# Token chunks of 512 instead of 470 in an FFT filter followed by a cosine-gated MLP (one core)

## The chip, the cores and the metric

The kernel runs on one core of one Trainium2 chip. The metric is the device time of one execution in microseconds (us); a smaller number is better. The engines of the core are called PE (TensorE matmul; PEld is its weight load), DVE (VectorE), ACT (ScalarE), POOL (GpSimd) and SP (SyncE, which issues most of the DMAs here).

## The reference

```python
# x: (8, 3008, 256); filt_r, filt_i: (1505, 256); w_in: (256, 2048); w_out: (2048, 256)
X = np.fft.rfft(x, axis=1)
Y = X * (filt_r + 1j * filt_i)[None, :, :]
y = np.fft.irfft(Y, n=3008, axis=1)          # circular filter along the sequence
t = y.reshape(8 * 3008, 256)                 # 24064 tokens
h = t @ w_in
out = (h * np.cos(h)) @ w_out                # (24064, 256), float32
```

## The kernel before

The work has two parts that are interleaved on all engines.

**The filter.** A sequence of 3008 = 47 * 64 positions is transformed by a prime-factor FFT in four stages. Stage 1 (`stage1`, L255) makes the transforms of length 47 and writes them to DRAM as `z1`. Stages 2 and 3 (`stage23`, L286) make the transforms of length 64 forward, multiply by the filter, and go back, to `z2` in DRAM. Stage 4 (`stage4`, L403) loads from `z2` the rows of some of the 64 values n2, multiplies them by a small matrix (L420) and combines even and odd parts (L427 to L429), which gives 47 tokens for each n2. The first sequence (batch 0) goes through faster code of its own (`first1`, `first23`), since nothing else can run before it; the other seven are spread under the second part.

**The MLP.** A chunk of tokens, held as two tiles `y` (a high part `yh`, L432, and the low rest `yl`, L435), goes through eight steps s. In a step, `hidden` (L441) makes 12 matmuls into the PSUM tile `hp`: 256 of the 2048 hidden values for all tokens of the chunk, with three products for each pair of tiles so that the precision is kept. `gate` (L457) then computes h * cos(h): L459 and L460 on DVE (a range reduction), L461 on ACT (a sine), L462 on DVE (the product, which is the last to read `hp`), L465 on ACT (the high part `gh`), L466 on POOL (the low part `gl`). `project` (L469) makes 12 matmuls of `gh` and `gl` into the two PSUM tiles `acc`, two steps after the `hidden` of the same step (`LAG`). After the eighth step L488 and L489 write the result out. A chunk has 470 tokens (five pairs of n2), the last two chunks 282 each: 52 chunks, 416 steps.

PSUM has two `hp` tiles, so the `hidden` of step k + 2 can't start before L462 of step k. The pool `moe` holds three buffers each of `g`, `gh` and `gl`; the pool `ypool` holds the tokens of two chunks.

**Order.** `run_due` hands out parts of the filter between the matmuls of the MLP by a table of due times, counted in slots (eight to a step, `SLOTS`). `LENGTH` slots are used for a sequence, which ends `BEFORE` slots ahead of its first chunk (`LATER` slots less for sequence 1, which can't begin before slot `FIRST`); `BEFORE4` says how far ahead of its use a part of stage 4 runs. A list scheduler of the framework then sets the order of each engine's instructions, and each engine works through its own in that order. The weights are converted on the way (`prep_w`, L199: an ACT instruction L216 after the load, a DVE instruction L219, POOL instructions L220 and L224); their loads stand in SP's queue among the others. Chunk 0 is reached by two parts of stage 4 that run before any MLP step.

Of the kernel before, what the change touches and what calls it, by code (L numbers as in the profile page):

```python
# [10 lines left out]
F32 = mybir.dt.float32  # L11
# [19 lines left out]
SLOTS = 8  # L31
LAG = 2
APART = 3
FIRST, LENGTH, BEFORE = 64, 410, 140
LATER = 28
GAP12, GAP23 = 20, 24
AHEAD1, AHEAD2, AHEAD4 = 28, 28, 24
BEFORE4 = 68
EARLY_W, JUST_W = 9, 5


# [104 lines left out]
def fft_filter_then_cos_glu(ctx: ExitStack, tc: tile.TileContext, ins, outT):
# [41 lines left out]
    chunks = _chunks()  # L188

    @contextmanager  # L190
    def behind():
# [52 lines left out]
    spare = []  # L244

    def psum_f(b):
        if b == 0 and len(done) < 2:
# [120 lines left out]
    def first23(i, fas, fbs):  # L368
        cols = slice(512 * i, 512 * i + 512)
        zf = fft.tile([P, 512], F32, name="zf", tag="ld", bufs=5)  # L370
        nc.sync.dma_start(zf, z1s[0].rearrange("j (h c k) d -> (j h c) (k d)", h=2, c=2)[:, cols])
        yield
        ps = psum_f(0)
        nc.tensor.matmul(ps, mats["f2"], zf, start=True, stop=True)
        half = slice(2 * (i % 2), 2 * (i % 2) + 2)
        ya = fft.tile([P, 512], F32, name="ya", bufs=2)
        yb = fft.tile([P, 512], F32, name="yb", tag="sw", bufs=2)
        for y, f in ((ya, fas), (yb, fbs)):
            nc.vector.tensor_tensor(y, ps, f[i // 2][:, half].rearrange("p k d -> p (k d)"), ALU.mult)
# [12 lines left out]
        to = z2[:NJ].rearrange("j (h c k) d -> (j h c) (k d)", h=2, c=2)[:, cols]  # L392
        n0 = 4 * chunks[0][1]
# [6 lines left out]
    ys = {}  # L400
    done = set()

    def stage4(c, half):  # L403


        j0, n = chunks[c]
        r, w = n * NK, n * Q
        rows = z2.rearrange("j q d -> (j q) d")[j0 * 2 * Q + half * w :][:w]
        zf = fft.tile([P, 2, D], F32, name="z4", tag="ld", bufs=5)[:r]
        load = nc.sync.dma_start(zf, rows.rearrange("(a p) d -> p a d", a=2))  # L410
        if c == 0:
            hold[:] = [load.ins]
        yield
        ps = psum_f(0 if c == 0 else 1)
# [7 lines left out]
        if c not in ys:  # L422
            ys[c] = [ypool.tile([P, NDT, 5 * TJ], F32R, name=f"y{i}") for i in range(2)]
        y = fft.tile([P, NDT, 5, NA], F32, name="y4", bufs=1)[:, :, :n]
        e = v.rearrange("p t (i g n) -> p t i g n", g=2, n=NK)
        odd = fft.tile([P, NDT, 5, NK], F32, name="odd", bufs=1)[:, :, :n]
        nc.scalar.copy(odd, e[:, :, :, 1])  # L427
        nc.vector.tensor_tensor(y[:, :, :, :NK], e[:, :, :, 0], odd, ALU.add)
        nc.vector.tensor_tensor(y[:, :, :, NK:], e[:, :, :, 0, 1:], odd[:, :, :, 1:], ALU.subtract)  # L429
        toks = slice(half * n * NA, (half + 1) * n * NA)  # L430
        yh, yl = (v[:, :, toks].rearrange("p t (i n) -> p t i n", n=NA) for v in ys[c])
        cast = nc.scalar.copy(yh, y)  # L432
        if (c, half) == (0, 1):
            hold.append(cast.ins)
        (nc.vector if c < 2 else nc.gpsimd).tensor_tensor(yl, y, yh.bitcast(F32), ALU.subtract)  # L435
        done.add((c, half))


    gs, accs = {}, {}

    def hidden(c, s):  # L441
        nt = chunks[c][1] * TJ
        yh, yl = ys[c]
        assert {(c, 0), (c, 1)} <= done
        hp = ps_h.tile([P, 2, 512], F32, name="hp")
        for u in range(2):
            fs = slice(u * P, (u + 1) * P)
            for t in range(NDT):
                for n, (w, y) in enumerate(((0, yh), (0, yl), (1, yh))):
                    nc.tensor.matmul(hp[:, u, :nt], w_in[s][w][:, t, fs], y[:, t, :nt],  # L450
                                     start=(t == 0 and n == 0), stop=(t == NDT - 1 and n == 2))
                if u == 0 or t == 0:
                    yield
        with tc.high_priority() if c == 0 else nullcontext():
            gs[c, s] = gate(hp[:, :, :nt], nt)

    def gate(h, nt):  # L457
        g = moe.tile([P, 2, 5 * TJ], F32, name="g")[:, :, :nt]
        nc.vector.tensor_scalar(g, h, 0.25, MAGIC, ALU.add, ALU.add)  # L459
        nc.vector.scalar_tensor_tensor(g, g, MAGIC, h, ALU.subtract, ALU.subtract)  # L460
        nc.scalar.activation(g, g, AF.Sin, bias=half_pi, scale=-TWO_PI)  # L461
        nc.vector.tensor_tensor(g, g, h, ALU.mult)  # L462
        gh = moe.tile([P, 2, 5 * TJ], F32R, name="gh")[:, :, :nt]
        gl = moe.tile([P, 2, 5 * TJ], F32R, name="gl")[:, :, :nt]
        nc.scalar.copy(gh, g)  # L465
        nc.gpsimd.tensor_tensor(gl, g, gh.bitcast(F32), ALU.subtract)  # L466
        return gh, gl

    def project(c, s):  # L469
        nt = chunks[c][1] * TJ  # L470
        if s == 0:
            accs[c] = [ps_o.tile([P, 512], F32, name=f"acc{e}") for e in range(2)]
        gh, gl = gs.pop((c, s))
        for e in range(2):
            acc = accs[c][e][:, :nt]
            es = slice(e * P, (e + 1) * P)
            for u in range(2):
                for n, (w, g) in enumerate(((0, gh), (1, gh), (0, gl))):
# [31 lines left out]
    with tc.tile_pool(name="first", bufs=12) as first, tc.manual_schedule(engines={mybir.EngineType.SP}):  # L510
# [47 lines left out]
    with tc.issue_after(hold[0]):  # L558
        for g in twos:
            next(g, None)  # L560
    steps = [(c, s) for c in range(len(chunks)) for s in range(NS)]

    due = []

# [18 lines left out]
            if pe:  # L583
                last[0] = now

    def slot(j):
        c = max(c for c in range(len(chunks)) if chunks[c][0] <= j)
        return SLOTS * NS * (c + (j - chunks[c][0]) / chunks[c][1])

    for b in range(1, B):  # L590
        end = slot(b * NJ) - BEFORE
        if b == 1:
            end += LATER
        start = max(end - LENGTH, FIRST)
# [7 lines left out]
    for c in range(1, len(chunks)):  # L602
        j0, n = chunks[c]
        for half in range(2):
            at = [SLOTS * NS * (c + (2 * half + t) / 4) - BEFORE4 for t in range(NDT)]
            b = (2 * j0 + (half + 1) * n - 1) // NB
            plan(stage4(c, half), at[0] - AHEAD4, at, lambda b=b: len(wrote2.get(b, ())) == n23)
    due.sort(key=lambda d: d[0])
    for k in range(len(steps) + LAG):
        parts = []  # L610
# [66 lines left out]
```

## Time and profile before

| | |
|---|---|
| median of 3 runs | 2503.86 us (2502.52 to 2504.66) |
| the profiled execution, its own time | 2502.54 us |
| its span, first to last instruction | 2500.4 us |
| mean granted TensorE clock | 0.992 |
| busy: PE, PEld, DVE, ACT, POOL | 2446.8, 2121.9, 1883.6, 1297.5, 1430.7 us |
| MLP matmuls | 9600 of 470 columns, 384 of 282 columns |
| gates | 400 of 128 x 940, 16 of 128 x 564 |

A line of the timeline shows a start time, the time taken, the engine, the source line and operation, output<-inputs by the program's names, shapes, how many were merged, and in brackets the idle time of the engine ahead of it with what ended it. Matmuls overlap, so what a matmul costs is read from the distance of starts and not from its own length.

### The profile page before, as it was taken

The numbers are of one execution on the slowest core, as the hardware profiler recorded it, in microseconds if no ns is written. First come the engines' busy times: TensorE is split into PE (matmuls) and PEld (weight loads), VectorE is DVE, ScalarE is ACT, GpSimd is POOL, SyncE is SP. The second block draws the span as 40 slices with busy tenths as digits, with TensorE's granted clock in tenths as the row PEclk, the third lists the DMA queues.
The fourth block names the chain that finished last, engine by engine and source line by source line (L and its number), as shares of the span: only waits on it lengthen the run. The fifth ranks groups of instructions, "written<-read, shape, count | busy, mean of one in ns | idle before, by whom it ended". The sixth has DMA issues, their size and how long they took to land.

```text
span 2500.4 us, 31920 instructions
## 1 busy us (share of the span) xinstructions
PE 2446.8 (98%) x11743; PEld 2121.9 (85%) x11743; DVE 1883.6 (75%) x2027; ACT 1297.5 (52%) x1751; POOL 1430.7 (57%) x824
## 2 busy tenths in 40 slices
PE   7799999999999999999999999999999999999999
PEld 2578888888888888888888888888888888888888
DVE  2688977887678866888678876788867886666665
ACT  1655554555555554555545564455554554444444
POOL 1776665665566555665556665556555654444444
PEclk8899999999999999999999999999999999999999
DMA  9633343323232132222322223222312221000000
GB/s 319 210 108 122 99 120 88 104 91 92 61 109 90 64 99 80 88 91 75 80 84 95 79 84 92 69 88 79 100 57 80 85 66 49 24 25 14 16 9 18
DMA packets 136301, 212.40 MB, mean 85 GB/s; under 512 B 12786, under 2 KB 77858, under 8 KB 136146
## 3 DMA queue, kind: packets, MB, share of 16 engines
q1 hardware_dynamic: 82526, 138.02, 18.2%
q10 hardware_dynamic: 53620, 72.34, 9.0%
q8 instruction: 94, 1.54, 0.3%
q14 instruction: 61, 0.50, 0.1%
HBM read 135.33 MB, written 74.97 MB: 84 GB/s over the span
## 4 chain that ended last, share of the span: by engine, by line
PE 87%; DVE 6%; DMA 3%; issue 2%; ACT 1%; POOL 1%; SPq 0%; ACTq 0%; POOLq 0%; DVEq 0%
PE hp L450 38%; PE acc L479 38%; PE ps L420 3%; PE ps L236 2%; PE ps L238 2%; PE ps L237 2%; DVE sw L310 1%; DVE g L460 1%; DVE g L459 1%; DVE g L462 1%; DMA zf<-z 1%; ACT g L461 1%; DVE zh L298 0%; DMA xf<-in_x 0%; PE hp L363 0%
## 5 line engine op out<-in xcount | busy, mean ns | idle before, releaser
L466 POOL TENSOR_TENSOR gl<-g,gh 128x940 fp32r<-128x940 f32 (+1 forms) x416 | 918.2, 2207 | 837.0 <-ACT gh L465 583.2
L450 PE MATMUL hp<-y,w_in 128*128 128x470 f32 (+1 forms) x4992 | 1135.1, 375 | 17.3 <-DVE g L462 14.5
L450 PEld LDWEIGHTS hp<-y,w_in 128*128 128x128 f32 x4992 | 925.0, 189 | 147.2 <-issue 9.9
L479 PE MATMUL acc<-gh,w_out 128*128 128x470 f32 (+1 forms) x3328 | 914.3, 373 | 0.3 <-ACT gh L465 0.3
L462 DVE TENSOR_TENSOR g<-g,hp 128x940 f32<-128x940 f32 (+1 forms) x416 | 463.9, 1115 | 335.0 <-ACT g L461 334.4
L479 PEld LDWEIGHTS acc<-gh,w_out 128*128 128x128 f32 x3328 | 619.5, 188 | 82.8 <-ACT gh L465 0.5
L461 ACT ACTIVATE g<-g,half_pi 128x940 f32<-128x940 f32 (+1 forms) x416 | 445.1, 1070 | 462.9 <-DVE g L460 427.6
L465 ACT CAST gh<-g 128x940 fp32r<-128x940 f32 (+1 forms) x416 | 402.1, 967 | 457.7 <-DVE g L462 445.3
L479 PE MATMUL acc<-gl,w_out 128*128 128x470 f32 (+1 forms) x1664 | 569.2, 377 | 4.2 <-POOL gl L466 4.2
L459 DVE TENSOR_SCALAR g<-hp 128x940 f32<-128x940 f32 (+1 forms) x416 | 464.2, 1116 | 112.1 <-PE hp L450 110.4
L460 DVE SCALAR_TENSOR_TENSOR g<-g,hp 128x940 f32<-128x940 f32 (+1 forms) x416 | 463.8, 1115 | 10.7
L479 PEld LDWEIGHTS acc<-gl,w_out 128*128 128x128 f32 x1664 | 311.9, 188 | 46.2 <-POOL gl L466 5.3
L316 POOL TENSOR_TENSOR yl<-ya,yh 128x512 fp32r<-128x512 f32 x84 | 113.5, 1351 | 54.7 <-ACT yh L315 53.4
L435 POOL TENSOR_TENSOR y<-y,y 128x470 fp32r<-128x470 f32 (+1 forms) x100 | 117.3, 1173 | 34.5 <-ACT y L432 34.3
L420 PEld LDWEIGHTS ps<-m,z 120*128 120x128 f32 (+1 forms) x824 | 125.9, 192 | 12.2
L299 POOL TENSOR_TENSOR zl<-zf,zh 128x512 fp32r<-128x512 f32 x84 | 111.4, 1327 | 38.5 <-DVE zh L298 17.0
L420 PE MATMUL ps<-m,z 120*128 120x120 f32 (+1 forms) x824 | 126.0, 273 | 0.0
L310 DVE SCALAR_TENSOR_TENSOR sw<-sw,sg,f 128x256 f32<-128x256 f32 x168 | 122.8, 770 | 0.0
L298 DVE CAST zh<-zf 128x512 fp32r<-128x512 f32 x84 | 99.5, 1184 | 19.8 <-DMA zf<-z 14.1
L315 ACT CAST yh<-ya 128x512 fp32r<-128x512 f32 x84 | 51.9, 617 | 81.7 <-DVE ya L312 80.7
L265 DVE TENSOR_TENSOR xo<-xf 120x512 f32<-120x512 f32 (+1 forms) x49 | 47.6, 973 | 53.2 <-DMA xf<-in_x 53.0
L312 DVE TENSOR_TENSOR ya<-ya,sw 128x512 f32<-128x512 f32 x84 | 80.6, 959 | 0.2
(96 smaller groups left out, 1409.8 us busy)
## 6 DMA issues: line engine op xcount, KB each, us to landing
z<-z SPq DMA_DIRECT2D x100, 240.0 KB
out_t<-o ACTq DMA_DIRECT2D x100, 235.0 KB
f<-in_fb SPq DMA_DIRECT2D x84, 256.0 KB
f<-in_fa SPq DMA_DIRECT2D x84, 256.0 KB
zf<-z SPq DMA_DIRECT2D x84, 256.0 KB
z<-z2t ACTq DMA_DIRECT2D x84, 256.0 KB
xf<-in_x SPq DMA_DIRECT2D x42, 480.0 KB
z<-z1t ACTq DMA_DIRECT2D x84, 240.0 KB
```

The lines of the kernel that those rows point to most:

```text
L310: nc.vector.scalar_tensor_tensor(sw[:, ks], sw[:, ks], sg[:, 2 * i + k : 2 * i + k + 1], fbt[:, ks], ALU.mult, ALU.mult)
L316: nc.gpsimd.tensor_tensor(yl, ya, yh.bitcast(F32), ALU.subtract)
L420: nc.tensor.matmul(v[:, t, a * r : (a + 1) * r], zf[:, a, t * P : (t + 1) * P], mats[f"m4{a}"][:r, :r], start=True, stop=True)
L435: (nc.vector if c < 2 else nc.gpsimd).tensor_tensor(yl, y, yh.bitcast(F32), ALU.subtract)
L450: nc.tensor.matmul(hp[:, u, :nt], w_in[s][w][:, t, fs], y[:, t, :nt], start=(t == 0 and n == 0), stop=(t == NDT - 1 and n == 2))
L459: nc.vector.tensor_scalar(g, h, 0.25, MAGIC, ALU.add, ALU.add)
L460: nc.vector.scalar_tensor_tensor(g, g, MAGIC, h, ALU.subtract, ALU.subtract)
L461: nc.scalar.activation(g, g, AF.Sin, bias=half_pi, scale=-TWO_PI)
L462: nc.vector.tensor_tensor(g, g, h, ALU.mult)
L465: nc.scalar.copy(gh, g)
L466: nc.gpsimd.tensor_tensor(gl, g, gh.bitcast(F32), ALU.subtract)
L479: nc.tensor.matmul(acc, w_out[s][w][:, u, es], g[:, u], start=(s == 0 and u == 0 and n == 0), stop=(s == NFT // 2 - 1 and u == 1 and n == 2))
```

## The change

The chunks get 512 tokens each, which is 24064 / 512 = 47 chunks and 376 steps, and all of them are of one size. The 47 tokens of an n2 no longer fit a chunk a whole number of times. So stage 4 goes in units of its own, which are runs of five n2 (235 tokens) wherever they lie; a unit that lies across two chunks writes its tokens in two pieces, with an ACT cast and a subtraction for each piece. Three units (5, 5 and 1 n2) now come before the first MLP step, since chunk 0 ends inside the third. `ypool` holds three chunks and `moe` two buffers of `g`, `gh` and `gl`. The numbers of the due table are other ones.

```diff
-FIRST, LENGTH, BEFORE = 64, 410, 140
-LATER = 28
-GAP12, GAP23 = 20, 24
-AHEAD1, AHEAD2, AHEAD4 = 28, 28, 24
-BEFORE4 = 68
+FIRST, LENGTH, BEFORE = 60, 376, 160
+LATER = 54
+GAP12, GAP23 = 20, 22
+AHEAD1, AHEAD2, AHEAD4 = 26, 26, 22
+BEFORE4 = 92
...
+def _units():
+    sizes = [5, 5, 1] + [5] * 99 + [3, 3]
...
+def _parts(u):
+    a, b = NA * u[0], NA * (u[0] + u[1])
+    return [(c, max(a, TC * c) - TC * c, min(b, TC * (c + 1)) - TC * c, max(a, TC * c) - a)
+            for c in range(a // TC, (b - 1) // TC + 1)]
...
-        cast = nc.scalar.copy(yh, y)
-        if (c, half) == (0, 1):
-            hold.append(cast.ins)
-        (nc.vector if c < 2 else nc.gpsimd).tensor_tensor(yl, y, yh.bitcast(F32), ALU.subtract)
+        for c, a, b, at in _parts(units[i]):
+            if c not in ys:
+                ys[c] = [ypool.tile([P, NDT, TC], F32R, name=f"y{k}") for k in range(2)]
+            yh, yl = (v[:, :, a:b] for v in ys[c])
+            part = flat[:, :, at : at + b - a]
+            cast = nc.scalar.copy(yh, part)
+            if i == n_first - 1 and c == 0:
+                hold.append(cast.ins)
+            (nc.vector if i < 2 * n_first else nc.gpsimd).tensor_tensor(yl, part, yh.bitcast(F32), ALU.subtract)
...
-                    nc.tensor.matmul(hp[:, u, :nt], w_in[s][w][:, t, fs], y[:, t, :nt],
+                    nc.tensor.matmul(hp[:, u], w_in[s][w][:, t, fs], y[:, t],
...
-    ypool = ctx.enter_context(tc.tile_pool(name="ypool", bufs=2, reuse_waits="tile"))
-    moe = ctx.enter_context(tc.tile_pool(name="moe", bufs=3, reuse_waits="tile"))
+    ypool = ctx.enter_context(tc.tile_pool(name="ypool", bufs=3, reuse_waits="tile"))
+    moe = ctx.enter_context(tc.tile_pool(name="moe", bufs=2, reuse_waits="tile"))
     with tc.high_priority():
-        for u in pipeline([lambda h=h: stage4(0, h) for h in range(2)], 3):
+        for u in pipeline([lambda i=i: stage4(i) for i in range(n_first)], 3):
...
-            at = [SLOTS * NS * (c + (2 * half + t) / 4) - BEFORE4 for t in range(NDT)]
+            at = [slot(NA * (k0 + n * t / NDT)) - BEFORE4 for t in range(NDT)]
```

The lines of the changed file lie 14 to 17 further down: L459, L460, L462 are L476, L477, L479; L461, L465, L466 are L478, L481, L483; L450 and L479 are L466 and L495; of the filter and the weights L219 is L234, L265 and L266 are L280 and L281, L298 is L313, L307, L310 and L312 are L322, L325 and L327, L428 and L429 are L442 and L443, L435 is L452.

The order of DVE's instructions moves at two places. The first is the start, from the stage-4 parts of chunk 0 (`y` and `odd` tiles) through the conversions of weights (`t<-o`) to the gates of the first MLP steps. Before:

```order
L428 TENSOR_TENSOR y_558<-ps,odd 128x10x24
L429 TENSOR_TENSOR y_558<-ps,odd 128x10x23
L435 TENSOR_TENSOR y_548<-y_558,y_547 128x2x235
L219 TENSOR_SCALAR t<-o 128x512 x2
L459 TENSOR_SCALAR g<-hp 128x940
L460 SCALAR_TENSOR_TENSOR g<-g,hp 128x940
L219 TENSOR_SCALAR t<-o 128x512
L459 TENSOR_SCALAR g<-hp 128x940
L462 TENSOR_TENSOR g<-g,hp 128x940
```

After:

```order
L442 TENSOR_TENSOR y_574<-hp,odd 128x2x24
L443 TENSOR_TENSOR y_574<-hp,odd 128x2x23
L452 TENSOR_TENSOR y_555<-y_574,y_554 128x2x42
L452 TENSOR_TENSOR y_582<-y_574,y_581 128x2x5
L234 TENSOR_SCALAR t<-o 128x512 x3
L476 TENSOR_SCALAR g<-hp 128x1024
L477 SCALAR_TENSOR_TENSOR g<-g,hp 128x1024
L476 TENSOR_SCALAR g<-hp 128x1024
L477 SCALAR_TENSOR_TENSOR g<-g,hp 128x1024
L479 TENSOR_TENSOR g<-g,hp 128x1024
```

The third unit's rows are added, the third weight conversion now stands ahead of the first gate where it stood behind that gate's second instruction, and the second gate's first two instructions now stand ahead of the first gate's last one.

The second place is DVE while sequence 1 is in stages 2 and 3 (`zh`, `ya`, `sw`) and sequence 2 begins with stage 1 (`xo`, `xf`), a few steps into the third chunk. Before, from the last instruction of one gate to that of the next:

```order
L462 TENSOR_TENSOR g<-g,hp 128x940
L459 TENSOR_SCALAR g<-hp 128x940
L312 TENSOR_TENSOR ya<-ya,sw 128x512
L460 SCALAR_TENSOR_TENSOR g<-g,hp 128x940
L298 CAST zh<-zf 128x512
L307 TENSOR_TENSOR ya<-ps,f 128x512
L310 SCALAR_TENSOR_TENSOR sw<-sw,sg,f 128x256 x2
L462 TENSOR_TENSOR g<-g,hp 128x940
```

After:

```order
L479 TENSOR_TENSOR g<-g,hp 128x1024
L327 TENSOR_TENSOR ya<-ya,sw 128x512
L477 SCALAR_TENSOR_TENSOR g<-g,hp 128x1024
L280 TENSOR_TENSOR xo<-xf 120x512
L281 TENSOR_TENSOR xf<-xf 120x512
L322 TENSOR_TENSOR ya<-ps,f 128x512
L325 SCALAR_TENSOR_TENSOR sw<-sw,sg,f 128x256 x2
L442 TENSOR_TENSOR y_2247<-ps,odd 128x10x24
L443 TENSOR_TENSOR y_2247<-ps,odd 128x10x23
L476 TENSOR_SCALAR g<-hp 128x1024
L479 TENSOR_TENSOR g<-g,hp 128x1024
```

In the stretch after, instructions of both sequences and of stage 4 stand between L477 and L479 of one gate, and the next gate's L476 has moved ahead of this gate's L479.

More of the change, by code (lines that the diff above doesn't have):

```diff
@@ L187, in fft_filter_then_cos_glu @@
     hold = []
-    chunks = _chunks()
+    units = _units()
+    of_chunk = [set() for _ in range(NC)]
+    for i, u in enumerate(units):
+        for c, *_ in _parts(u):
+            of_chunk[c].add(i)
+    n_first = len(of_chunk[0])
     @contextmanager
@@ L246, in psum_f @@
     def psum_f(b):
-        if b == 0 and len(done) < 2:
+        if b == 0 and len(done) < n_first:
             if not spare:
@@ L392, in first23 @@
         to = z2[:NJ].rearrange("j (h c k) d -> (j h c) (k d)", h=2, c=2)[:, cols]
-        n0 = 4 * chunks[0][1]
+        n0 = 2 * units[n_first][0]
         nc.scalar.dma_start(to[:n0], z[:n0])
@@ L401, in fft_filter_then_cos_glu, with stage4 @@
     done = set()
-    def stage4(c, half):
-        j0, n = chunks[c]
+    def stage4(i):
+        k0, n = units[i]
         r, w = n * NK, n * Q
-        rows = z2.rearrange("j q d -> (j q) d")[j0 * 2 * Q + half * w :][:w]
+        rows = z2.rearrange("j q d -> (j q) d")[k0 * Q : k0 * Q + w]
         zf = fft.tile([P, 2, D], F32, name="z4", tag="ld", bufs=5)[:r]
         load = nc.sync.dma_start(zf, rows.rearrange("(a p) d -> p a d", a=2))
-        if c == 0:
+        if i < n_first:
             hold[:] = [load.ins]
         yield
-        ps = psum_f(0 if c == 0 else 1)
+        ps = psum_f(0 if i < n_first else 1)
         v = ps[:, : 2 * w].rearrange("p (t n) -> p t n", t=NDT)
@@ L421, in stage4 @@
                                  mats[f"m4{a}"][:r, :r], start=True, stop=True)
-        if c not in ys:
-            ys[c] = [ypool.tile([P, NDT, 5 * TJ], F32R, name=f"y{i}") for i in range(2)]
-        y = fft.tile([P, NDT, 5, NA], F32, name="y4", bufs=1)[:, :, :n]
+        flat = fft.tile([P, NDT, 5 * NA], F32, name="y4", bufs=1)
+        y = flat[:, :, : n * NA].rearrange("p t (i n) -> p t i n", n=NA)
         e = v.rearrange("p t (i g n) -> p t i g n", g=2, n=NK)
@@ L429, in stage4 @@
         nc.vector.tensor_tensor(y[:, :, :, NK:], e[:, :, :, 0, 1:], odd[:, :, :, 1:], ALU.subtract)
-        toks = slice(half * n * NA, (half + 1) * n * NA)
-        yh, yl = (v[:, :, toks].rearrange("p t (i n) -> p t i n", n=NA) for v in ys[c])
-        cast = nc.scalar.copy(yh, y)
-        if (c, half) == (0, 1):
-            hold.append(cast.ins)
-        (nc.vector if c < 2 else nc.gpsimd).tensor_tensor(yl, y, yh.bitcast(F32), ALU.subtract)
-        done.add((c, half))
+        for c, a, b, at in _parts(units[i]):
[7 more added lines that the diff above has]
+            (nc.vector if i < 2 * n_first else nc.gpsimd).tensor_tensor(yl, part, yh.bitcast(F32), ALU.subtract)
+        done.add(i)
     gs, accs = {}, {}
     def hidden(c, s):
-        nt = chunks[c][1] * TJ
         yh, yl = ys[c]
-        assert {(c, 0), (c, 1)} <= done
+        assert of_chunk[c] <= done
         hp = ps_h.tile([P, 2, 512], F32, name="hp")
@@ L474, in project @@
         for e in range(2):
-            acc = accs[c][e][:, :nt]
+            acc = accs[c][e]
             es = slice(e * P, (e + 1) * P)
@@ L560, in fft_filter_then_cos_glu @@
             next(g, None)
-    steps = [(c, s) for c in range(len(chunks)) for s in range(NS)]
+    steps = [(c, s) for c in range(NC) for s in range(NS)]
     due = []
@@ L584, in run_due, with slot @@
                 last[0] = now
-    def slot(j):
-        c = max(c for c in range(len(chunks)) if chunks[c][0] <= j)
-        return SLOTS * NS * (c + (j - chunks[c][0]) / chunks[c][1])
+    def slot(n):
+        return SLOTS * NS * n / TC
     for b in range(1, B):
-        end = slot(b * NJ) - BEFORE
+        end = slot(b * S) - BEFORE
         if b == 1:
@@ L601, in fft_filter_then_cos_glu @@
             plan(stage23(b, i), t - AHEAD2, [t, t + GAP23], lambda b=b: len(wrote1.get(b, ())) == 2 * n1)
-    for c in range(1, len(chunks)):
-        j0, n = chunks[c]
-        for half in range(2):
-            at = [SLOTS * NS * (c + (2 * half + t) / 4) - BEFORE4 for t in range(NDT)]
-            b = (2 * j0 + (half + 1) * n - 1) // NB
-            plan(stage4(c, half), at[0] - AHEAD4, at, lambda b=b: len(wrote2.get(b, ())) == n23)
+    for i, (k0, n) in enumerate(units):
+        if i >= n_first:
+            at = [slot(NA * (k0 + n * t / NDT)) - BEFORE4 for t in range(NDT)]
+            plan(stage4(i), at[0] - AHEAD4, at, lambda b=(k0 + n - 1) // NB: len(wrote2.get(b, ())) == n23)
     due.sort(key=lambda d: d[0])
```

26 lines of the change are left out of this document (12 added, 14 removed).

## The prediction

> **What bounds the kernel now.** I read the page's busy line first, then the busy time by stretches. In the rows of stretches the numbers behind each length are the busy us of PE, PEld, DVE, ACT and POOL, then the granted clock.
>
> ```profile
> PE 2446.8 (98%) x11743; PEld 2121.9 (85%) x11743; DVE 1883.6 (75%) x2027; ACT 1297.5 (52%) x1751; POOL 1430.7 (57%) x824
> ```
> ```profile
> 86.00:100.00 14.00, 8.44 (x29) 6.98 (x30) 7.66 (x10) 8.11 (x14) 7.93 (x7) 0.74 0.95 343
> 100.00:200.00 100.00, 93.99 (x446) 80.13 (x445) 83.01 (x82) 58.19 (x86) 77.53 (x45) 0.99 0.43 119
> 200.00:300.00 100.00, 96.21 (x457) 82.87 (x456) 92.72 (x103) 56.76 (x82) 66.48 (x40) 1.00 0.38 123
> ...
> 400.00:1000.00 600.00, 599.63 (x2900) 525.94 (x2899) 468.24 (x511) 322.83 (x437) 358.74 (x207) 1.00 0.29 89
> ```
>
> From 400 us on, PE is busy for 599.63 of 600 us: the end is set by the number of matmuls and their pace, and nothing that DVE, ACT or POOL do can shorten it. Only before 400 us does PE wait: 5.6 us of the 14 behind the first MLP step, 6.0 us in 100 to 200, 3.8 us in 200 to 300, where DVE is busy for 92.72 of 100. So three questions decide: the pace at 512 columns, the start, and the crowded stretch.
>
> **The pace.** Starts of matmuls in the timeline: an undisturbed stretch of 470 columns, two runs of six filter matmuls of 512 columns (first of the run, and the one that follows it), and a step of the last chunk with 282.
>
> ```profile
> 2332.09 2.74 PE L450 MATMUL hp<-y,w_in 128*128 128x470 f32 x12
> ...
> 2347.49 1.67 PE L450 MATMUL hp<-y,w_in 128*128 128x470 f32 x7
> ```
> ```profile
> 151.58 0.39 PE L236 MATMUL ps<-xh,m1e 120*120 120x512 f32 x1
> ...
> 152.98 0.38 PE L479 MATMUL acc<-gl,w_out 128*128 128x470 f32 x1
> ...
> 157.81 0.39 PE L236 MATMUL ps<-xh,m1e 120*120 120x512 f32 x1
> ...
> 159.20 0.60 PE L479 MATMUL acc<-gh,w_out 128*128 128x470 f32 x2
> ```
> ```profile
> 2452.14 1.72 PE L450 MATMUL hp<-y,w_in 128*128 128x282 f32 x12
> ...
> 2455.26 1.74 PE L450 MATMUL hp<-y,w_in 128*128 128x282 f32 x12
> ```
>
> Between 2332.09 and 2347.49 lie three steps of 24: 15.40 / 72 = 213.9 ns for 470 columns. Six of 512 take 1.40 and 1.39 us: 233.3 and 231.7, mean 232.5 ns. For 282 columns 3.12 / 24 = 130.0 ns. The line through 282 and 470 meets 512 at 232.6, so I take 232.5. Nearly all of it goes with the columns, and the columns do not change; only some 5 ns of each matmul are saved, 960 times over.
>
> Before: 400 steps * 5.133 + 16 * 3.12 = 2103.1 us. After: 376 * 24 * 0.2325 = 2098.1 us. **Term 1: -5.0 us.** The ends: at 231.7 ns it is -12.2, at 233.3 ns +2.2. In plain proportion to the columns (233.0 ns) it would be -0.4.
>
> The Trainium skill ("TensorE: Matmul & The Clock Gate", section "Back-to-back issue gap") gives N / 2.4 + 2.5 ns for the isolated gap of a warm matmul. By that 470 columns take 198.3 ns and 512 take 215.8, and an estimate from it for term 1 is -2.4 us; the rows above disagree with its level by 8%, so the rows decide.
>
> **The gates.** Line, operation and shapes; busy us and mean ns of one:
>
> ```profile
> L459 DVE TENSOR_SCALAR g<-hp 128x940 f32<-128x940 f32 x400 | 452.3, 1131 | 105.2 <-PE hp L450 103.4 <-POOL xl L272 0.7
> ...
> L459 DVE TENSOR_SCALAR g<-hp 128x564 f32<-128x564 f32 x16 | 11.9, 743 | 7.0 <-PE hp L450 7.0
> ```
> ```profile
> L466 POOL TENSOR_TENSOR gl<-g,gh 128x940 fp32r<-128x940 f32 x400 | 895.7, 2239 | 807.5 <-ACT gh L465 556.6 <-issue 150.7 <-DVE g L459 26.7
> ...
> L466 POOL TENSOR_TENSOR gl<-g,gh 128x564 fp32r<-128x564 f32 x16 | 22.5, 1407 | 29.5 <-ACT gh L465 26.6 <-issue 1.7 <-PE acc L479 1.2
> ```
>
> On the line through both widths a DVE instruction of a gate takes 1.22 us at 1024 and POOL's 2.43. There are 40 gates fewer and the sums fall a little, beside PE: nothing on the path. The same holds for the additional casts and subtractions of units that lie across two chunks (some 46 of each): ACT and POOL are idle for over 40% of the span. Stage 4 keeps its 416 matmuls. With a third token buffer a cast of tokens no longer waits for an old chunk, which costs or saves PE nothing while it is busy. All this is costed at 0, with PE's own work as the cover; where the cover is thin, the next two terms have it.
>
> **The start.** Timeline from the token casts of chunk 0 to the third MLP step:
>
> ```profile
> 82.78 0.59 ACT L432 CAST y<-y 128x470 fp32r<-128x470 f32 x1 [0.78 <-DVE y L429]
> ...
> 85.13 0.58 ACT L432 CAST y<-y 128x470 fp32r<-128x470 f32 x1 [0.99 <-DVE y L429]
> ...
> 85.77 6.83 PE L450 MATMUL hp<-y,w_in 128*128 128x470 f32 x24 [2.46 <-ACT y L432]
> ...
> 90.28 1.14 DVE L459 TENSOR_SCALAR g<-hp 128x940 f32<-128x940 f32 x1 [1.57 <-PE hp L450]
> ...
> 94.66 0.66 ACT L216 ACTIVATE o<-raw 128x512 f32<-128x512 f32 x1 [3.86 <-DMA raw<-in_w_out]
> ...
> 95.42 0.43 DVE L219 TENSOR_SCALAR t<-o 128x512 int32<-128x512 int32 x1 [2.83 <-ACT o L216]
> ...
> 95.76 1.13 DVE L459 TENSOR_SCALAR g<-hp 128x940 f32<-128x940 f32 x1
> ...
> 96.87 1.13 DVE L462 TENSOR_TENSOR g<-g,hp 128x940 f32<-128x940 f32 x1
> ...
> 98.15 4.84 PE L450 MATMUL hp<-y,w_in 128*128 128x470 f32 x12 [5.56 <-DVE g L462]
> ```
>
> Two things get longer. A third stage-4 unit goes through ACT and DVE one behind the other. A full unit follows the one before at 85.13 - 82.78 = 2.35 us; the third has a fifth of the elements, so it costs between 0.5 and 2.35 us, and I take 1.4, nearer the small end.
>
> Then DVE's order. The third weight conversion (95.42, waiting for a load that landed at 94.6) now stands ahead of the first gate, whose first instruction ran at 90.28. Behind it come four instructions of two gates and only then the product that frees `hp`. From 95.85 on that is five instructions of 1.22 us, less some overlap: it ends near 101.7 in place of 98.0, so PE goes on 3.7 us later, less 0.4 us because 24 wider matmuls lie behind it. Queued behind that wait on DVE are the gates alone; PE waits for them. The load has one more DMA ahead of it in SP's queue, the third unit's, which may add 0.4.
>
> Together 4.7 to 5.1 us. Not all of it lasts: PE loses another 6.0 us between 100 and 200 us, and the chain of waits goes there through work that does not start later because PE does, as this load of stage 1:
>
> ```profile
> 167.15 4.01 DMA xf<-in_x
> ```
>
> A late PE finds part of such waits over. The ends are 0 and 5.1; I take the nearer third. **Term 2: +1.5 us.** In the row for 86 to 100 the granted clock is 0.74, and the 12 matmuls at 98.15 take 4.84 us against 2.74 in the undisturbed stretch, so a longer wait can also cost half-speed matmuls behind it: up to 2 us more, kept for the range.
>
> **The crowded stretch.** While sequence 1 is in stages 2 and 3 and sequence 2 begins, DVE has more to do than PE. By the due numbers the two overlap for 28 slots before (the end at 297 slots, the start at 269) and for 54 slots after (270 and 216). The groups' means, and what PE waits for:
>
> ```profile
> L310 DVE SCALAR_TENSOR_TENSOR sw<-sw,sg,f 128x256 f32<-128x256 f32 x168 | 122.8, 770 | 0.0
> ...
> L298 DVE CAST zh<-zf 128x512 fp32r<-128x512 f32 x84 | 99.5, 1184 | 19.8 <-DMA zf<-z 14.1 <-PE ps L237 5.3
> ...
> L312 DVE TENSOR_TENSOR ya<-ya,sw 128x512 f32<-128x512 f32 x84 | 80.6, 959 | 0.2
> ...
> L307 DVE TENSOR_TENSOR ya<-ps,f 128x512 f32<-128x512 f32 x84 | 57.5, 685 | 9.7 <-ACT sw L305 8.7
> ...
> L265 DVE TENSOR_TENSOR xo<-xf 120x512 f32<-120x512 f32 x42 | 41.0, 977 | 50.4 <-DMA xf<-in_x 50.1
> ...
> L428 DVE TENSOR_TENSOR y<-ps,odd 128x240 f32<-128x240 f32 x99 | 39.6, 400 | 4.4 <-POOL y L435 3.5 <-ACT odd L427 0.2
> ```
> ```profile
> PE hp L450 <- DVE g L462: 14.5, 14, 5.6
> ```
>
> Counted in the order, between the products of gates 16 and 24 before, DVE has 24 gate instructions, 9 of L298, 6 of L307, 12 of L310, 5 of L312 and 6 of L428 and L429: 58.3 us; the eight steps of PE that answer to them have 192 MLP and 38 filter matmuls (six of half width; stage 4's small ones left out here and below), 49.3 us. The excess is 9.0 us on paper (neighbours overlap a little), and 3.8 us were lost. After, between the products of gates 16 and 28, there are 37, 9, 12, 24, 11 and 8, and 7 of stage 1: 103.0 us against 86.9 of PE, an excess of 16.1. Scaled as before, 3.8 * 16.1 / 9.0 = 6.8 us are lost. **Term 3: +3.0 us**, between 0 (all absorbed by the deeper lead of stage 4) and +7.1 (the whole difference of the excesses).
>
> **Sum.** -5.0 + 1.5 + 3.0 = -0.5 us against the profiled execution's 2502.54, so 2502.0. The median of the runs is 1.3 us higher, which makes 2503.4.
>
> **Rivals.**
>
> *Faster: the offsets do not last.* PE already idles in the start and in the crowded stretch; if a late start is absorbed there and only the pace is left, the time moves by -5.0 to -9 (the pace's end is -12.2), to some 2497. For it: PE is saturated from 400 on, so whatever the pace gives arrives at the end. Against it: both offsets are read from an order in which DVE waits at a named place.
>
> *Slower: two gate buffers.* An undisturbed gate before, and the step two further on:
>
> ```profile
> 2334.94 1.14 DVE L459 TENSOR_SCALAR g<-hp 128x940 f32<-128x940 f32 x1 [0.50 <-PE hp L450]
> ...
> 2338.45 1.13 DVE L462 TENSOR_TENSOR g<-g,hp 128x940 f32<-128x940 f32 x1 [1.21 <-ACT g L461]
> ...
> 2340.78 2.23 POOL L466 TENSOR_TENSOR gl<-g,gh 128x940 fp32r<-128x940 f32 x1 [2.93 <-ACT gh L465]
> ...
> 2342.35 2.74 PE L450 MATMUL hp<-y,w_in 128*128 128x470 f32 x12
> ...
> 2345.20 1.14 DVE L459 TENSOR_SCALAR g<-hp 128x940 f32<-128x940 f32 x1 [0.48 <-PE hp L450]
> ```
>
> With two buffers L459 of a step must wait until POOL has read `g` two steps back: POOL is done at 2343.0, L459 starts at 2345.20, 2.2 us to spare (2.5 when scaled to 512). Behind it PE has 2.8 us between the product's end (2339.58) and the `hidden` that needs it (2342.35). So POOL must be over 5 us late. One of its filter instructions takes 1.35 us, so it takes four of them ahead of a gate's:
>
> ```profile
> L316 POOL TENSOR_TENSOR yl<-ya,yh 128x512 fp32r<-128x512 f32 x84 | 113.5, 1351 | 54.7 <-ACT yh L315 53.4 <-PE hp L450 1.3
> ```
>  In the order 38 of 376 steps have three or more others ahead of POOL's gate instruction, against 15 of 416. If each of the 38 cost PE 0.3 us, the time is 2503.4 + 11 = 2514.
>
> *The width gives nothing.* At 233.0 ns (plain proportion) term 1 is -0.4 and the sum +4.1: 2508.
>
> **Chances.** The forecast 0.55 (own range 2499 to 2508), faster rival 0.28, two buffers 0.12, no gain from width 0.05. About 0.2%, 5 us, is what can be told from no change: faster 0.31, same 0.53, slower 0.16. The range 2495 to 2511 reaches into both sides.
>
> **What would show it.** Right: MLP matmuls 232 to 233 ns apart; the third step's first matmul near 102 us, its wait ended by the gate's product; PE losing some 6 to 7 us between 190 and 280 us with DVE over 95% busy; PE over 99.5% busy from 400 on. Wrong: PE waits spread over the whole span with POOL's gate instruction behind L476 (the second rival), or a pace under 231 or over 234 ns.

## The result and the profile after

The changed kernel takes 2559.56 us (median of 4 runs, 2558.91 to 2562.1) against 2504.26 us of the kernel before on the same chip: a ratio of 1.0222 [1.0204, 1.0239], some 55 us slower. The forecast was 2503.4 us in a range of 2495 to 2511, with no rival above 2514. It was wrong by far more than any of its terms. One of all the executions reported below, of `both_edits`, was slow (2988.39 us at a granted clock of 0.75): it is in that kernel's median and not in its ratio.

The busy line of the page after, and the shares of the chain of waits by engine (the chain goes back from the last instruction, at each step to what that one waited for):

```profile
PE 2455.7 (96%) x10783; PEld 1967.7 (77%) x10783; DVE 1885.4 (74%) x1911; ACT 1286.1 (50%) x1707; POOL 1430.5 (56%) x826
```
```profile
PE 82%; DVE 7%; DMA 3%; issue 3%; SPq 2%; ACT 2%; POOL 1%; POOLq 0%; ACTq 0%; DVEq 0%
```

Apart from the weight loads (PEld), which are fewer, the busy times are within 1% of those before, so what grew is waiting. The rows of stretches say where (columns as in the prediction):

```profile
86.00:100.00 14.00, 8.27 (x24) 6.21 (x24) 2.02 (x7) 3.90 (x8) 5.05 (x4) 0.74 0.13 51
100.00:200.00 100.00, 50.32 (x205) 39.47 (x206) 54.23 (x54) 37.83 (x59) 48.72 (x29) 0.73 0.43 129
200.00:300.00 100.00, 97.64 (x441) 78.57 (x440) 83.87 (x86) 53.21 (x75) 65.78 (x40) 1.00 0.36 110
300.00:400.00 100.00, 86.14 (x350) 66.22 (x349) 86.10 (x87) 55.35 (x82) 61.49 (x38) 0.93 0.44 133
400.00:1000.00 600.00, 599.21 (x2693) 487.67 (x2692) 470.15 (x481) 320.36 (x429) 358.49 (x210) 1.00 0.28 85
```

The last row but one was, before:

```profile
300.00:400.00 100.00, 98.08 (x469) 85.19 (x468) 77.27 (x80) 55.80 (x78) 62.60 (x37) 1.00 0.36 103
```

Between 100 and 200 us PE is busy for 50.32 us where it was 93.99, between 300 and 400 for 86.14 where it was 98.08. From 100 to 136 us PE, DVE, ACT and POOL are all idle, so it is no engine's work. The chain of waits has 2% for SP's queue (SPq), where it had 0%. The timeline of that queue before, and then after:

```profile
78.59 0.40 SPq L207 DMA_DIRECT2D raw<-in_w_in  x1
79.04 10.15 SPq L397 DMA_DIRECT2D z<-z2t  x12
89.29 0.56 SPq L207 DMA_DIRECT2D raw<-in_w_out  x1
```
```profile
78.62 0.40 SPq L222 DMA_DIRECT2D raw<-in_w_in  x1
79.06 43.36 SPq L412 DMA_DIRECT2D z<-z2t  x12
122.52 4.30 SPq L222 DMA_DIRECT2D raw<-in_w_out  x1
```

The twelve DMAs that write the rest of `z2t` for the first sequence begin at the same time, and SP needs 43.36 us in place of 10.15 to issue them. The weight load behind them leaves 33 us later, and ACT can start on it 14.0 us after its issue, where it was 5.4 (why the load itself took longer has not been settled). What sets the rows of the twelve is a line of the diff that the excerpt ahead of the prediction left out:

```diff
-        n0 = 4 * chunks[0][1]
+        n0 = 2 * units[n_first][0]
         nc.scalar.dma_start(to[:n0], z[:n0])
...
         nc.sync.dma_start(to[n0:], z[n0:])
```

With three early units `n0` is 22 in place of 20, and the rest has 106 rows in place of 108. The DMA views of the two stretches, before (79 to 90 us) and after (90 to 122 us), packets with sizes, and queue 1 with its share of 16 engines:

```profile
DMA packets 1809, 3.26 MB, mean 297 GB/s; under 512 B 156, under 2 KB 281, under 8 KB 1808
...
q1 hardware_dynamic: 1808, 3.26, 84.8%
```
```profile
DMA packets 813, 1.64 MB, mean 51 GB/s; under 512 B 14, under 2 KB 14, under 8 KB 813
...
q1 hardware_dynamic: 813, 1.64, 13.1%
```

13.1% of 16 engines is 2.1 engines, at 51 GB/s; before it was 13.6 engines at 297 GB/s. The rest follows in order: ACT's first step of the third weight conversion, DVE's, the first gate behind it, the product that frees `hp`, the third MLP step.

```profile
136.55 0.66 ACT L231 ACTIVATE o<-raw 128x512 f32<-128x512 f32 x1 [44.14 <-DMA raw<-in_w_out]
...
137.32 0.43 DVE L234 TENSOR_SCALAR t<-o 128x512 int32<-128x512 int32 x1 [46.97 <-ACT o L231]
137.66 1.22 DVE L476 TENSOR_SCALAR g<-hp 128x1024 f32<-128x1024 f32 x1
...
142.44 1.21 DVE L479 TENSOR_TENSOR g<-g,hp 128x1024 f32<-128x1024 f32 x1
...
143.80 4.58 PE L466 MATMUL hp<-y,w_in 128*128 128x512 f32 x12 [48.24 <-DVE g L479]
```

All of these are held by one load that is late; the gates stand behind its conversion in DVE's order.

### The profile page after: what moved, and what is told of

Its sections match the earlier page's. It is cut to its first block, busy times and chain, and to the rows that moved or that the text cites. A ratio compares the mean times of both kernels' runs of the same rounds, so it can differ in the third digit from the quotient of the medians.

```text
span 2560.3 us, 29873 instructions
## 1 busy us (share of the span) xinstructions
PE 2455.7 (96%) x10783; PEld 1967.7 (77%) x10783; DVE 1885.4 (74%) x1911; ACT 1286.1 (50%) x1707; POOL 1430.5 (56%) x826
## 4 chain that ended last, share of the span: by engine, by line
PE 82%; DVE 7%; DMA 3%; issue 3%; SPq 2%; ACT 2%; POOL 1%; POOLq 0%; ACTq 0%; DVEq 0%
PE hp L466 36%; PE acc L495 36%; PE ps L435 3%; PE ps L251 2%; PE ps L252 2%; PE ps L253 2%; SPq L412 2%; DVE g L476 1%; DMA xf<-in_x 1%; DVE sw L325 1%; DVE g L477 1%; DMA raw<-in_w_in 1%; ACT g L478 1%; DVE g L479 1%; DVE xo L280 1%
## 5 line engine op out<-in xcount | busy, mean ns | idle before, releaser
L483 POOL TENSOR_TENSOR gl<-g,gh 128x1024 fp32r<-128x1024 f32 x376 | 910.7, 2422 | 825.6 <-ACT gh L481 510.7
L466 PE MATMUL hp<-y,w_in 128*128 128x512 f32 x4512 | 1132.6, 400 | 65.8 <-DVE g L479 63.8
L466 PEld LDWEIGHTS hp<-y,w_in 128*128 128x128 f32 x4512 | 845.3, 190 | 266.6 <-issue 59.8
L495 PE MATMUL acc<-gh,w_out 128*128 128x512 f32 x3008 | 896.9, 396 | 0.7 <-ACT gh L481 0.7
L479 DVE TENSOR_TENSOR g<-g,hp 128x1024 f32<-128x1024 f32 x376 | 457.9, 1218 | 320.6 <-ACT g L478 320.1
L478 ACT ACTIVATE g<-g,half_pi 128x1024 f32<-128x1024 f32 x376 | 433.4, 1153 | 484.2 <-DVE g L477 436.6
L495 PEld LDWEIGHTS acc<-gh,w_out 128*128 128x128 f32 x3008 | 564.0, 188 | 131.1 <-ACT gh L481 1.1
L481 ACT CAST gh<-g 128x1024 fp32r<-128x1024 f32 x376 | 394.9, 1051 | 430.5 <-DVE g L479 424.1
L476 DVE TENSOR_SCALAR g<-hp 128x1024 f32<-128x1024 f32 x376 | 458.8, 1220 | 137.7 <-PE hp L466 130.3
L495 PE MATMUL acc<-gl,w_out 128*128 128x512 f32 x1504 | 549.9, 400 | 1.3 <-POOL gl L483 1.3
L477 DVE SCALAR_TENSOR_TENSOR g<-g,hp 128x1024 f32<-128x1024 f32 x376 | 458.0, 1218 | 9.9
L495 PEld LDWEIGHTS acc<-gl,w_out 128*128 128x128 f32 x1504 | 283.7, 189 | 66.7 <-POOL gl L483 2.1
L452 POOL TENSOR_TENSOR y<-y,y 128x470 fp32r<-128x470 f32 (+29 forms) x142 | 124.9, 884 | 55.8 <-ACT y L449 55.8
L435 PEld LDWEIGHTS ps<-m,z 120*128 120x128 f32 (+1 forms) x816 | 129.3, 192 | 21.0
L435 PE MATMUL ps<-m,z 120*128 120x120 f32 (+1 forms) x816 | 129.2, 273 | 0.0
L325 DVE SCALAR_TENSOR_TENSOR sw<-sw,sg,f 128x256 f32<-128x256 f32 x168 | 116.9, 735 | 0.0
L313 DVE CAST zh<-zf 128x512 fp32r<-128x512 f32 x84 | 93.1, 1108 | 23.1 <-DMA zf<-z 13.4
L327 DVE TENSOR_TENSOR ya<-ya,sw 128x512 f32<-128x512 f32 x84 | 98.5, 1173 | 0.0
```

Of the source, the lines that this page charges most:

```text
L325: nc.vector.scalar_tensor_tensor(sw[:, ks], sw[:, ks], sg[:, 2 * i + k : 2 * i + k + 1], fbt[:, ks], ALU.mult, ALU.mult)
L452: (nc.vector if i < 2 * n_first else nc.gpsimd).tensor_tensor(yl, part, yh.bitcast(F32), ALU.subtract)
L466: nc.tensor.matmul(hp[:, u], w_in[s][w][:, t, fs], y[:, t], start=(t == 0 and n == 0), stop=(t == NDT - 1 and n == 2))
L495: nc.tensor.matmul(acc, w_out[s][w][:, u, es], g[:, u], start=(s == 0 and u == 0 and n == 0), stop=(s == NFT // 2 - 1 and u == 1 and n == 2))
```

## The experiments

To sum up each run I use one number: what PE loses, which is the distance from each matmul's start to the next one's less the undisturbed distance of its shape, summed over a stretch (half-speed matmuls are in it). For the profiled executions, in us:

| kernel | rest rows | span | lost 0 to 200 | lost 200 to 400 | lost from 400 |
|---|---|---|---|---|---|
| before | 108 | 2500.4 | 67.1 | 7.7 | 10.4 |
| after | 106 | 2560.3 | 112.7 | 25.3 | 9.2 |
| before_22rows | 106 | 2558.5 | 108.6 | 22.9 | 11.6 |
| after_24rows | 104 | 2517.2 | 70.5 | 23.7 | 10.0 |
| after_32rows | 96 | 2514.6 | 70.8 | 18.4 | 13.0 |
| after_98rows | 98 | 2517.8 | 70.7 | 25.5 | 8.2 |
| after_92rows | 92 | 2521.8 | 89.3 | 10.1 | 9.7 |
| conversion_behind_gate | 104 | 2511.1 | 67.3 | 17.3 | 14.0 |
| second_sequence_late | 104 | 2502.5 | 69.2 | 7.5 | 12.2 |
| both_edits | 104 | 2504.0 | 64.8 | 13.7 | 12.5 |
| late_second_and_first | 104 | 2512.3 | 68.0 | 18.2 | 12.6 |
| before_two_gate_buffers | 108 | 2505.6 | 67.3 | 10.9 | 11.7 |
| before_96_rows | 96 | 2509.8 | 68.3 | 14.1 | 11.8 |

After against before: 45.6 + 17.6 - 1.2 and the pace (-2.8, below) make 59.2 of the span's 59.9.

**Is it the rows? `after_24rows`.** The instructions of PE, DVE and POOL stand in the order of the changed kernel (on ACT two change places, at 75 us); by hand only the split of the rows differs.

```diff
-        n0 = 2 * units[n_first][0]
+        n0 = 24
```

> The changed kernel with one number altered: of the first sequence's rows in z2, ACT's early DMA takes the first 24 and SP's later one the other 104, where it was 22 and 106. The order of all engines' instructions stays as it is. Theory A (the rest rows' DMAs are spread badly): with 106 rows each of the twelve DMAs (L412) holds SP for a median 4.36 us and all of them for 43.36 us, against 10.15 us for 108 rows before; the weight load behind them lands 42 us late and DVE's order makes PE wait for it. With 104 rows SP's twelve take 10 to 13 us, the third MLP step starts at 100 to 106 us, and the time is 2559.6 - 35 to 45 = 2515 to 2525 us; what is left over 2504 is the crowded stretch (some 22 us of PE waits between 280 and 400 us against 8 before). Theory B (it is the order: a third unit, an additional DMA in SP's queue and a third weight conversion ahead of the first gate, whatever the row count): SP's twelve stay above 35 us and the time stays above 2550 us.

Measured: 2519.25 us, ratio 1.0062 [1.0048, 1.0076].

```profile
79.66 10.16 SPq L412 DMA_DIRECT2D z<-z2t  x12
89.92 0.51 SPq L222 DMA_DIRECT2D raw<-in_w_out  x1
```
```profile
95.33 0.66 ACT L231 ACTIVATE o<-raw 128x512 f32<-128x512 f32 x1 [2.28 <-DMA raw<-in_w_out]
...
102.58 4.70 PE L466 MATMUL hp<-y,w_in 128*128 128x512 f32 x12 [6.68 <-DVE g L479]
```

Two rows fewer, and the twelve issues take 10.16 us in place of 43.36. ACT's step and PE's third step are each 41.2 us earlier, and the time falls by 40.3. So the split of the rows makes 40 us of the 55. The other 15 us are a second question.

**The same in the kernel before: `before_22rows`.**

```diff
-        n0 = 4 * chunks[0][1]
+        n0 = 22
```

> The kernel before with the same one number: 22 early rows and 106 rest rows where it was 20 and 108. Theory A: SP's twelve DMAs (L397) take 40 to 45 us in place of 10.15, the third MLP step starts near 133 us in place of 98, and the time is 2504 + 30 to 40 = 2534 to 2544 us. Theory B: within 5 us of 2504, since nothing of the new order is in it.

Measured: 2558.78 us, ratio 1.0219 [1.0205, 1.0233].

```profile
80.76 43.30 SPq L397 DMA_DIRECT2D z<-z2t  x12
124.15 3.67 SPq L207 DMA_DIRECT2D raw<-in_w_out  x1
```

106 rows alone make the kernel before as slow as the changed one. The 30 to 40 us that were expected are too few: besides 41.5 us in the first 200, 15.2 more are lost from 200 to 400. From the late step on, the list scheduler set the instructions in another order here, so the second number is not the late load alone.

**What about 106? `after_98rows`, `after_92rows` and `after_32rows`.** `n0` is 30, 36 and 32. 98 rows keep the order of PE, DVE and POOL; 92 and 96 do not.

> The changed kernel with 98 rest rows (the early part writes 30), everything else in the same order. It asks what made 106 rows slow. Theory (a DMA is cut over as many engines as divide its rows, up to 16): 98 = 14 * 7 rows, 14 engines, so SP's twelve issues take 9 to 11 us and the time is 2516 to 2521, as with 104. Rival (106 is slow because it is no multiple of 4; 98 is none either): they take 35 to 43 us and the time is 2545 to 2560.

> The changed kernel with 92 rest rows (the early part writes 36): fewer bytes than 104 and a multiple of 4. Theory (engines by the divisor of the rows): 92 = 4 * 23, so 4 engines with 23 rows of 2 KB each; at the 82 ns of a row that 106 rows showed (4.357 us for 53) one DMA takes 1.9 us and the twelve issues 18 to 23 us, the load behind them is issued 8 to 12 us later than with 104, and the time is 2525 to 2535. Rival (number of bytes, or multiples of 4): the issues take 8 to 10 us and the time is 2515 to 2521.

> The changed kernel with 32 early rows and 96 rest rows. Theory A with the count of row groups as the reason (104 = 13 * 8, 96 = 16 * 6): SP's twelve take as long as with 104 rows or 1 to 3 us less, and the time is within 3 us of the kernel with 24 early rows. If only the number of rows counted (fewer rows, less time in proportion), the twelve would take 43.36 * 96 / 106 = 39 us and the time would stay above 2550.

Measured: 98 rows 2518.32 us, 1.0059 [1.0044, 1.0074]; 92 rows 2523.49, 1.0085 [1.007, 1.01]; 96 rows 2517.48, 1.0055 [1.0042, 1.0069]. SP's queue and queue 1 with 98 rows, then with 92:

```profile
79.83 9.58 SPq L412 DMA_DIRECT2D z<-z2t  x12
```
```profile
q1 hardware_dynamic: 1671, 2.96, 94.5%
```
```profile
80.04 18.15 SPq L412 DMA_DIRECT2D z<-z2t  x12
```
```profile
q1 hardware_dynamic: 755, 1.46, 27.3%
```

98 is no multiple of 4 and is fast; 92 has fewer bytes than 104, is a multiple of 4, and is slow: 27.3% of 16 is 4.4 engines. What fits all runs is the largest number up to 16 that divides the rows: 106 gives 2, 92 gives 4, 104 gives 13, 98 gives 14, 108 gives 12, 96 gives 16 (twelve issues in 8.31 us). This is what the Trainium skill states ("DMA: Bandwidth & Descriptors", section "Why a DMA increments its semaphore by 16 and not by 1": a DMA uses the largest k up to 16 that divides the slowest dimension of both sides) and the trace agrees: 2.1 engines' time for 106 rows and 4.4 for 92, where almost nothing but these DMAs ran; 13.6 for 108 and 15.1 for 98, with other transfers beside them. With 92 rows the twelve issues took 18.15 us where 18 to 23 were expected. The time came out below its 2525: 18.8 us more than with 104 rows were lost in the first 200, but 13.6 less from 200 to 400 (10.1), in another order of instructions.

**Two gate buffers, the slower rival of the prediction: `before_two_gate_buffers`.**

```diff
-    moe = ctx.enter_context(tc.tile_pool(name="moe", bufs=3, reuse_waits="tile"))
+    moe = ctx.enter_context(tc.tile_pool(name="moe", bufs=2, reuse_waits="tile"))
```

> The kernel before with two buffers of g, gh and gl in place of three, nothing else by hand. Theory (spare time is enough): an undisturbed gate has 2.2 us to spare, then 2.8 us more until PE notices; 2504 + 0 to 4 us, PE waits between 400 and 2400 us stay under 15 us. Rival (the second rival of the prediction): each gate with three or more other POOL instructions ahead of it costs PE 0.3 us or more: 2510 or more, the waits spread over the whole span.

Measured: 2505.79 us, ratio 1.0008 [0.9999, 1.0017]. From 400 us on PE loses 11.7 us against 10.4. In the kernel with 470 columns the third buffer is worth nothing that can be told, and the changed kernel, which has two, loses 9.2 us there; the rival falls.

**The other 15 us: `conversion_behind_gate`, `second_sequence_late`, `both_edits`.** By the table 104 rows lose 3.4 us more than before in the first 200 us and 16.0 more between 200 and 400. One edit is made for each. The first ties the conversion behind the first gate's second instruction, the second starts sequence 2 later; both rest on `after_24rows`.

```diff
-        nc.vector.scalar_tensor_tensor(g, g, MAGIC, h, ALU.subtract, ALU.subtract)
+        frac = nc.vector.scalar_tensor_tensor(g, g, MAGIC, h, ALU.subtract, ALU.subtract)
+        if len(hold) == 2:
+            hold.append(frac.ins)
...
+        with tc.issue_after(hold[-1]):
             next(g, None)
```
```diff
-        start = max(end - LENGTH, FIRST)
+        start = max(end - LENGTH + (36 if b == 2 else 0), FIRST)
```

> The changed kernel with 104 rest rows (2519.25 us), and the third weight conversion tied behind the second instruction of the first gate, where it stands in the kernel before. It tests the order's share of the start. Theory (DVE's order holds the third step): the third step's first matmul is at 98.5 to 99.5 us in place of 102.58, its wait of 6.68 us becomes about 3, PE loses 14 to 15 us between 100 and 200 us in place of 18.3, and the time is 2514 to 2517. Rival (the crowded stretch sets the pace behind it and absorbs it): the third step is as early, but the time stays within 2518 to 2521.

> The changed kernel with 104 rest rows (2519.25 us), and sequence 2 started 36 slots later with the same end, so that it overlaps sequence 1 for 18 slots in place of 54 (28 in the kernel before). It tests the crowded stretch. Theory (the overlap makes DVE late, and waits of over 2 us bring half-speed matmuls): PE loses under 12 us between 200 and 400 us in place of 23.7, and the time is 2506 to 2512. Rival (what is lost there comes from the late start or from the longer gates, not from the overlap): 18 us or more are still lost, and the time is 2515 to 2521.

> Both edits at once: 104 rest rows, the conversion behind the first gate, sequence 2 started 36 slots later. Theory (start and overlap are two separate costs): the gains add, some -4 and -10 from 2519.25, so 2502 to 2508, level with the kernel before (2504.7). Rival (one of them only makes room for the other's wait): no more than the better of the two alone, 2509 to 2517.

Measured: 2507.97 us, ratio 1.0021 [1.0012, 1.0031]; 2505.44 us, 1.0006 [0.9997, 1.0016]; both 2510.16 us, 1.0022 [1.0012, 1.0031], against 2503.55 for the kernel before. (The 18.3 us "between 100 and 200" of the first expectation, and the 9.4 of the kernel before that a later one sets beside such a figure, are not alike: the wait ahead of the third step is in the first, and just outside the second, where that step begins at 98.15. The table's 0 to 200 has it in both.)

The first edit on DVE and PE:

```profile
91.64 1.23 DVE L476 TENSOR_SCALAR g<-hp 128x1024 f32<-128x1024 f32 x1 [1.75 <-PE hp L466]
...
94.94 0.43 DVE L234 TENSOR_SCALAR t<-o 128x512 int32<-128x512 int32 x1 [0.82 <-ACT o L231]
```
```profile
97.83 5.46 PE L466 MATMUL hp<-y,w_in 128*128 128x512 f32 x12 [3.67 <-DVE g L481]
```

The third step comes 4.75 us earlier, 1.1 us of it because its first step began earlier, and 3.2 us are won in the first 200 as the prediction's 3.7 for DVE's order had it. The medians differ by 11.3 us, where 2 to 5 were expected. The profiled execution, at 2512.9 us the slowest of its ten, is only 6.1 us below that with 104 rows: 3.2 us are won in the first 200, 6.4 from 200 to 400, where the instructions stand in another order too, and 4.0 are lost behind that. What makes the other 5 us of the median is not shown.

The second edit in the rows of stretches, with 104 rows as it was and with sequence 2 late:

```profile
200.00:300.00 100.00, 90.98 (x393) 71.61 (x392) 86.16 (x94) 54.02 (x80) 64.51 (x40) 0.95 0.42 134
300.00:400.00 100.00, 95.08 (x405) 75.59 (x405) 77.32 (x73) 53.09 (x74) 58.42 (x35) 0.96 0.32 92
```
```profile
200.00:300.00 100.00, 96.84 (x431) 76.71 (x430) 91.91 (x97) 57.02 (x81) 67.28 (x41) 1.00 0.40 125
300.00:400.00 100.00, 98.36 (x433) 78.81 (x432) 75.79 (x78) 55.38 (x78) 62.52 (x37) 1.00 0.38 106
```

With the overlap of 54 slots cut to 18, the loss falls from 23.7 to 7.5 us, the level before (7.7), with the instructions in the same order up to 250 us, and the time falls by 13.8. So the 15 us lie in this stretch, and in the trace with 104 rows all of PE's waits there end on DVE. That the length of the overlap alone sets the loss is not shown: with 92 rows and the same 54 slots it is 10.1 us, in `before_22rows` with 28 slots 22.9, in `both_edits` with 18 slots 13.7, each in another order of instructions.

DVE was not busy all that time. With 104 rows:

```profile
262.89 1.78 DVE L280 TENSOR_TENSOR xo<-xf 120x512 f32<-120x512 f32 x1 [3.17 <-DMA xf<-in_x]
...
292.82 1.57 DVE L280 TENSOR_TENSOR xo<-xf 120x512 f32<-120x512 f32 x1 [1.40 <-DMA xf<-in_x]
```

Ahead of three of the four waits of PE of over 1.8 us there (those that end at 266, 296 and 343 us), DVE sat idle for 3.17, 1.40 and 2.69 us until a load of stage 1 landed, and what PE needed stood behind that in DVE's order. With sequence 2 late, DVE has no such wait of over 0.8 us between 200 and 299 us.

Part of the loss is speed and not idle time. With 104 rows again:

```profile
266.12 0.50 PE L251 MATMUL ps<-yh,m 128*128 128x512 f32 x1 [2.15 <-DVE ya L322]
...
269.79 4.74 PE L466 MATMUL hp<-y,w_in 128*128 128x512 f32 x12 [0.55 <-DVE g L479]
```

PE waits 2.15 us, the granted clock is 0.50 from 266.67 to 273.50 us, and the next 12 matmuls of a step take 4.74 us where the same twelve take 2.96 undisturbed. Counting all that follow at 1.6 to 2.15 times the usual distance, 26 matmuls cost 5.0 us between 200 and 400 us here, 4 cost 0.6 with the late sequence, and 1 costs 0.2 before.

The two edits together do not add; the rival was right that the sum gains no more than the better of the two alone. The start is the best of all (64.8), but 13.7 us are lost in the crowded stretch, in yet another order of instructions, and this trace is of the fastest of the ten executions (2505.84 us). Why that order is worse has not been settled.

**Two attempts to gain on it: `late_second_and_first` and `before_96_rows`.** The first is `second_sequence_late` with sequence 1 started later as well:

```diff
-FIRST, LENGTH, BEFORE = 60, 376, 160
+FIRST, LENGTH, BEFORE = 68, 376, 160
```

> The changed kernel with 104 rest rows and sequence 2 started 36 slots later (2505.44), and sequence 1 started at slot 68 in place of 60 (64 in the kernel before) with the same end. It asks whether what PE still loses between 100 and 200 us (17.5 us against 9.4 before) comes from sequence 1 meeting the weight conversions. Theory (it does): under 13 us are lost there, and the time is 2499 to 2503, ahead of the kernel before. Rival (the start loses them by the order of conversions and gates alone, and a denser sequence 1 gives the rest back): 2504 to 2509.

> The kernel before with 96 rest rows in place of 108 (the early part writes 32 rows). It asks whether SP's twelve DMA issues bind the kernel before as well. Theory (they do, by the load behind them): the twelve issues take 8 us in place of 10.15, the load is issued 2 us earlier, the third step begins near 96 us in place of 98.15, and the time is 2502 to 2503.5. Rival (at 10 us they are hidden): 2504 to 2505.5.

Measured: 2514.06 us, 1.0045 [1.0029, 1.0062]: the first 200 us gain 1.2 and the next 200 give back 10.7, more than the rival said. And the kernel before with `n0 = 32`: 2511.18 us, 1.0026 [1.0017, 1.0035].

```profile
79.09 8.52 SPq L397 DMA_DIRECT2D z<-z2t  x12
```
```profile
97.80 6.72 PE L450 MATMUL hp<-y,w_in 128*128 128x470 f32 x23 [2.97 <-DVE g L462]
```

SP is 1.6 us quicker, the third step 0.35 us earlier, and yet the kernel is 7.6 us slower; neither theory fits. The list scheduler set the instructions after the start in another order, and 14.1 us are lost from 200 to 400 in place of 7.7. That the order is the reason is argued, not shown. No version ran ahead of the kernel before.

## Why the prediction was wrong, and where it was right

- **The step that failed** is in "The start": "The load has one more DMA ahead of it in SP's queue, the third unit's, which may add 0.4." The load is the right one and PE does wait for it in the way described, but ahead of it stand also the twelve DMAs of the rest rows, and the change made them 106 rows long. In the runs SP needed 43.36 us for these twelve in place of 10.15, and that step cost 40.3 us (`after` against `after_24rows`) in place of 0.4. The line with `n0` was in the diff and was given no price; DMAs that a change reshapes were counted only in number.
- **The start without it** was put at +1.5 us with ends of 0 and 5.1; it is +3.4 (70.5 against 67.1), inside. The third step "near 102 us", held by the gate's product, is at 102.58 in `after_24rows`. Tying the conversion back gave 3.2 of the 3.7 us that its order was said to cost.
- **The crowded stretch** was mis-sized: 6.8 us lost and +3.0 forecast, 23.7 lost and +16.0 measured with 104 rows, far over the upper bound of 7.1. That PE would wait for DVE there was right. But the count took DVE to be short of time, over 95% busy, and scaled its excess as if waits were spread evenly. DVE was busy for 86.16 of 100 us, less than before; it waited for loads of stage 1 itself, PE's waits behind that were some 2 us long, and half-speed matmuls made 5.0 us of the loss. How much of the rest is the overlap and how much the order stays open.
- **The pace** was nearly right. A step in the last stretch of the changed kernel:

```profile
2440.73 2.96 PE L466 MATMUL hp<-y,w_in 128*128 128x512 f32 x12
...
2474.33 2.96 PE L466 MATMUL hp<-y,w_in 128*128 128x512 f32 x12
```

  Six steps in 33.60 us are 233.3 ns; the mean of all undisturbed distances is 232.99 ns, against 214.07 (470 columns) and 130.9 (282) before. 376 * 24 * 232.99 ns less 9600 * 214.07 and 384 * 130.9 ns gives -2.8 us where the term was -5.0: 232.5 was read from two runs of six, and the 213.9 and 130.0 of the kernel before were a little low as well. The estimate from the rule N / 2.4 + 2.5 of the Trainium skill ("TensorE: Matmul & The Clock Gate", section "Back-to-back issue gap", where it is for the isolated gap) was -2.4, nearer than my term, though the measured 232.99 ns lie 8% above the 215.8 it gives for 512 columns.
- **From 400 us on** PE is busy for 599.21 of 600 us: right. The gates cost nothing there, and the rival of the two gate buffers falls.
- **The faster rival** (offsets are absorbed) is refuted where it counts: in `after_24rows` an added 3.4 us of start was not absorbed in the crowded stretch, which lost 16.0 more itself.

## What to carry to other kernels

When a change alters how many rows a DMA has, look at the divisors of that number before anything else: 106 rows, with the divisor 2, had the time of 2.1 engines, and the price, 40 us, was paid by the next load in the same queue. Price each DMA that a diff reshapes, also where it only gets smaller. Where two engines are close to each other's pace, a count of busy time misses the waits of the engine that is counted: +3.0 us on paper was +16.0 here. And a change of a few numbers rearranges what follows, so that one edit's gain can't be added to another's.

## What was not expected of the hardware

A DMA on few engines holds up the issuing queue: with 106 rows an issue on SP took 4.36 us (median of the twelve) against 0.65 with 108 and 104 rows, and 53 rows of 2 KB for each of two engines in that time are 82 ns a row. TensorE's half speed came back after a wait of 2.15 us in the middle of dense work. In the trace with 104 rows it followed waits of 2.15, 2.28 and 1.94 us between 200 and 400 us, but not one of 2.28 us that ended at 141.46.
